# Queries and keys for the block-turned tiles fetched as four consecutive tokens per partition

## The chip, the cores and the metric

The kernel runs on one core of a Trainium2 chip. The metric is device microseconds for one launch. Three runs of the kernel before took 568.88, 570.08 and 571.22 us; the median is 570.08 us. Engines are called by the names of the profile: PE (matrix products; PEld is its weight load), DVE, ACT, POOL, and SP, which here only issues transfers.

## The reference

Eight batches of 576 tokens, eight heads, head width 64. Attention is causal with a window of 128 tokens, a linear distance penalty per head, scale 1/8. Its output, laid out as tokens by 512 features, goes through a gated layer: `h = relu(x @ w_in)` with 1,024 features, a three-tap convolution of `h` along the tokens, `gate = sigmoid(conv)`, and `(h * gate) @ w_out`.

```
scores = scale * q @ k.T ; scores + slope_h * (-|i - j|) where 0 <= i - j < 128, else -1e9
attn   = softmax(scores) ; x = (attn @ v) as [batch, token, head * 64]
h      = max(x @ w_in, 0)
conv   = sum over k of conv_w[k] * h shifted by k - 1 tokens
out    = (h * sigmoid(conv)) @ w_out
```

## The kernel before

All 4,608 tokens are one row of 36 tiles of 128 tokens. A batch has four and a half tiles, so tiles 4, 13, 22 and 31 hold the end of one batch and the start of the next. For tiles 0 to 8 the queries and keys are turned (feature to partition) on PE. For tiles 9 to 35 (`TURN = 9`) they are turned on DVE in blocks of 32 by 32, and the change touches these alone.

For such a tile the steps are, with their names in the written-out order:

- `LD`, `load` and `load_blocks` (lines 281 to 301): SP fetches queries and keys into `raws[t]`. Partition `32 * h + r` of a group of four heads holds, for each of the four blocks `m` of 32 tokens, the 64 features of token `32 * m + r` of head `h`. One transfer per tensor, group and block: 128 pieces of 256 bytes, 16 transfers a tile. Three buffers hold `raws`.
- `TQ`, `turn` (line 348): DVE turns all 32 by 32 blocks, giving `blks[t]`, in which the free index of a row runs over the tile's 128 tokens in order.
- `HQ`, `qk_hi` (line 361): ACT writes the rounded part of all 1,024 values per partition to `qkT`.
- `LQ`, `qk_lo` (line 368): POOL (DVE for tiles 9 and 10) writes what the rounding left to `qkT_low`.
- `S`, `scores_blocks` (line 387): PE forms the scores from `qkT` and `qkT_low`.

Behind them on the engines come: on POOL the normalisation `N` (line 508), `XL` (line 658, which the next up-projection `UH`, line 698, reads), the halves of the gate `GL` (line 767), and the masks `CE` (lines 569, 573) of the probabilities, which go by way of DRAM: `TE` (line 541, DVE), `WE` (line 550, SP writes), `SE` (line 561, SP reads back), `CE`, and then `AV` (line 592) on PE.

The order on every engine, SP among them, is written out by hand: an opening, thirteen periods of two tiles each (tiles 8 and 9, 10 and 11, up to 34; the first at t = 8), a tail. In a period for tiles t and t + 1 SP runs `LD5` (tile t + 5), `WE2`, `SE1`, `SE2`, the values' loads, `LD6`, output stores and `WE3`. `TQ3 HQ3 LQ3` and `TQ4 HQ4 LQ4` prepare tiles t + 3 and t + 4, and `S3.0`, `S4.0` use them in the same period. An engine takes its instructions strictly in this order.

Of the kernel before, what the change touches and what calls it, by code (L numbers as in the profile page):

```python
# [14 lines left out]
ALU = mybir.AluOpType  # L15

P = 128
# [5 lines left out]
def tile_alibi_window_attention_conv_glu(  # L23
# [10 lines left out]
    nc = tc.nc  # L34
# [21 lines left out]
    def as32(ap):  # L56
        return ap.bitcast(F32)
# [21 lines left out]
    def mask_from(name, conds):  # L79
# [19 lines left out]
        out=mh, in_=mh, pattern=[[0, P]], compare_op=ALU.is_ge, fill=0.0, base=-(P // 2), channel_multiplier=1  # L99
# [13 lines left out]
        out=dist, in0=m_prev_f, scalar=float(P), in1=dist, op0=ALU.mult, op1=ALU.add  # L113
# [4 lines left out]
    for h in range(H):  # L118
        slope = 2.0 ** (-8.0 * (h + 1) / H)
        nc.vector.tensor_scalar(  # L120
            out=bias[:, h, :], in0=dist, scalar1=-8.0 * slope, scalar2=None, op0=ALU.mult
# [127 lines left out]
    qkT_low = cpool.tile([P, SLOTS, 2, 2, NG, P], F32R, name="qkT_low")  # L249
    qkTs = {}  # L250

    def qkT_of(t):
        kind = F32 if t < SPLIT else F32R
        if kind not in qkTs:
            qkTs[kind] = apool.tile([P, SLOTS, 2, 2, NG, P], kind, name=f"qkT{t}", tag="qkT", bufs=1)
        return qkTs[kind]
# [11 lines left out]
    def segments(t):  # L268
        g, end = t * P, (t + 1) * P
        while g < end:  # L270
            b, s = divmod(g, S)
            n = min(end - g, S - s)
            yield g - t * P, b, s, n
            g += n

    TURN = 9
    BK = 32
    NB = P // BK
    blks = {}

    def load_blocks(t, dst, src):
        for r, b, s, n in segments(t):
            for g in range(NG):
                for m in range(0, n, BK):
                    nc.sync.dma_start(
                        out=dst[:, g, (r + m) // BK],
                        in_=src[b, g * NB : (g + 1) * NB, s + m : s + m + BK, :],
                    )

    def head_of(t, i):  # L290
        return i if t < TURN else i % 2 + 2 * (i // HU) + NB * (i // 2 % 2)
# [4 lines left out]
    def load(t):  # L296
        if t >= TURN:
            raws[t] = apool.tile([P, 2, NG, NB, D], F32, name=f"rqk{t}", tag="rqk", bufs=3)
            for i, src in enumerate((q, k)):
                load_blocks(t, raws[t][:, i], src)  # L300
            return
        rqk = apool.tile([P, 2, H, D], F32, name=f"rqk{t}", tag="rqk", bufs=3)
        for dst, src in ((rqk[:, 0], q), (rqk[:, 1], k)):
            fetch(t, dst, src)
        raws[t] = [rqk]
# [37 lines left out]
    def turn(t):  # L343
# [6 lines left out]
            in_=raws[t].rearrange("p i g m (b r) -> p (i g) m b r", r=BK),  # L350
        )

    def turned_of(x, t):
        return x[:, t % SLOTS].rearrange("p u i g k -> p (u i g k)").rearrange(
            "p (i g b k) -> p i g b k", i=2, g=NG, k=P
        )

    def qk_hi(t):
        if t < TURN:
            return  # L360
        nc.scalar.copy(out=turned_of(qkT_of(t), t), in_=blks[t])  # L361

    def qk_lo(t):
        if t < TURN:
            return
        hi = as32(turned_of(qkT_of(t), t))
        eng = nc.vector if t in LQ_DVE else nc.gpsimd
        eng.tensor_tensor(out=turned_of(qkT_low, t), in0=blks[t], in1=hi, op=ALU.subtract)  # L368

    def scores_blocks(t):  # L370
        first, slot, win, prev, cur = window(t)
# [456 lines left out]
    def qk_rest(t):  # L828
# [4 lines left out]

    TILE = {
        "LD": load, "LH": load_half, "QU": qkT, "QV": qkT_out, "LV": loadv, "Q": qk, "QO": qk_out, "QL": qk_rest, "QM": qkT_rest, "TE": turn_e, "WE": write_e, "SE": swap_e, "CE": select_e, "TQ": turn, "HQ": qk_hi, "LQ": qk_lo, "MP": place, "MB": add_bias, "KH": keys_hi, "KL": keys_low, "KT": keys_top, "S": scores, "MA": merge,
        "X": lambda t, u, h: exps(t, u, range(h, HU, 2)),
        "NR": recips, "N": normal, "T": attnT, "RL": attn_out, "SEL": select, "AV": av, "XA": x_part, "XS": x_sum, "XH": x_hi, "XL": x_lo, "XF": xfin,
# [107 lines left out]
```

## Time and profile before

| what | value |
|---|---|
| three runs, median | 570.08 us |
| the profiled execution, its own time | 568.98 us |
| its span (first to last instruction) | 567.3 us |
| PE busy | 558.1 us, 98% |
| DVE, ACT, POOL busy | 82%, 76%, 70% |
| hardware transfer queue, share of the 16 engines | 51.6% |

The span is what the trace covers; the profiled execution's own time is 1.7 us longer. A busy share is a mean over the opening, the periods and the tail, and each of them has to be looked at by itself. A group of instructions is told by its line, its engine and the tiles that it writes and reads.

### The profile page before, as it was taken

To read this page: it belongs to the slowest core of one execution; us is meant where nothing else is said; L and a number is where in the kernel's file an instruction comes from. 1 tells how busy PE (TensorE), PEld (TensorE's weight loads), DVE (VectorE), ACT (ScalarE), POOL (GpSimd) and SP (SyncE) were. 2 spreads that over 40 slices of the span, in tenths; PEclk is the share of its full clock that TensorE was granted. 3 is DMA by queue.
4 is the path that set the end of the run, shared out by engine and by line. 5 is a ranking of instruction groups with operands and counts; after the bars stand their busy time and mean duration, and the time that the engine had idled before them with its cause. 6 is when DMAs were issued, how large, how long until landed. Compare 5 with 4: busy or idle time off the path is not lost.

```text
span 567.3 us, 16990 instructions
## 1 busy us (share of the span) xinstructions
PE 558.1 (98%) x6121; PEld 490.0 (86%) x6121; DVE 463.2 (82%) x1474; ACT 430.6 (76%) x1225; POOL 394.8 (70%) x453
## 2 busy tenths in 40 slices
PE   9889999999999999999999999999999999999997
PEld 7667878788989898989898998989898989899996
DVE  7899999999889987888778877788879987765444
ACT  6899988777777878778777877777876888664463
POOL 2667677777878787778677778777677878564141
PEclk9899999999999999999999999999999999999999
DMA  8996813325656474747484647474746462630001
GB/s 196 260 251 138 258 36 76 99 70 160 134 156 139 131 164 125 175 121 173 124 177 124 172 125 174 125 175 125 174 123 171 125 171 79 150 112 25 16 11 66
DMA packets 141225, 76.63 MB, mean 135 GB/s; under 512 B 116412, under 2 KB 131028, under 8 KB 141140
## 3 DMA queue, kind: packets, MB, share of 16 engines
q1 hardware_dynamic: 141140, 75.55, 51.6%
q8 instruction: 48, 0.79, 0.6%
q14 instruction: 37, 0.30, 0.2%
HBM read 51.40 MB, written 24.12 MB: 133 GB/s over the span
## 4 chain that ended last, share of the span: by engine, by line
PE 91%; DVE 4%; DMA 2%; issue 1%; SPq 1%; ACT 0%; DVEq 0%
PE o L801 34%; PE p L698 34%; PE sc L387 8%; PE av L592 7%; PE o L791 2%; DMA rqk<-in_k_dram 2%; PE sc L432 2%; DVE sc L458 1%; PE av L632 1%; PE p L693 1%; SPq L320 1%; DVE wg L216 1%; PE pt L330 1%; DVE e L476 1%; DVE low L209 0%
## 5 line engine op out<-in xcount | busy, mean ns | idle before, releaser
L698 PE MATMUL p<-ring,wi 128*128 128x256 f32 x1088 | 195.4, 281 | 0.0
L731 DVE SCALAR_TENSOR_TENSOR zp<-hh,cw,zp 128x256 f32<-128x256 f32 (+7 forms) x384 | 160.5, 418 | 41.5 <-ACT zp L716 34.0
L698 PEld LDWEIGHTS p<-ring,wi 128*128 128x128 f32 x1088 | 168.7, 188 | 3.3 <-issue 0.2
L698 PE MATMUL p<-ring,wl 128*128 128x256 f32 x544 | 152.3, 280 | 0.0
L767 POOL TENSOR_TENSOR gl<-z,gh 128x512 fp32r<-128x512 f32 x67 | 86.8, 1296 | 79.9 <-ACT gh L758 79.1
L484 ACT ACTIVATE e<-e,st 128x128 f32<-128x128 f32 x288 | 112.7, 394 | 17.7 <-DVE st L476 17.4
L801 PE MATMUL o<-wo,gh 128*128 128x512 f32 x270 | 110.3, 409 | 0.0
L801 PE MATMUL o<-wo,gl 128*128 128x512 f32 x270 | 105.7, 392 | 0.0
L801 PE MATMUL o<-wl,gh 128*128 128x512 f32 x270 | 105.6, 391 | 0.0
L698 PEld LDWEIGHTS p<-ring,wl 128*128 128x128 f32 x544 | 102.7, 189 | 0.0
L716 ACT ACTIVATE zp<-hh,cw 128x256 f32<-128x256 f32 x144 | 68.9, 478 | 30.8 <-DVE z L746 20.2
L508 POOL TENSOR_TENSOR e<-e,st 128x512 f32<-128x512 f32 x60 | 62.4, 1041 | 15.1 <-DVE st L496 14.9
L368 POOL TENSOR_TENSOR qkT_low<-blk,qkT 128x1024 fp32r<-128x1024 f32 x25 | 59.9, 2397 | 16.8 <-ACT qkT L361 10.5
L476 DVE CUSTOM_DVE_ANT_0 e<-sc,bias 128x128 f32<-128x128 f32 x288 | 69.0, 285 | 1.1 <-DVE sc L458 0.2
L738 ACT ACTIVATE zp<-zp 128x512 f32<-128x512 f32 (+1 forms) x73 | 42.1, 577 | 33.3 <-DVE zp L731 33.1
L801 PEld LDWEIGHTS o<-wo,gh 128*128 128x128 f32 x270 | 50.6, 187 | 13.8 <-issue 0.2
L746 DVE SCALAR_TENSOR_TENSOR z<-zp,hh 128x512 f32<-128x512 f32 (+1 forms) x73 | 49.3, 676 | 14.1 <-ACT zp L738 12.3
L801 PEld LDWEIGHTS o<-wo,gl 128*128 128x128 f32 x270 | 50.6, 187 | 11.6
L710 ACT ACTIVATE hh<-p 128x512 f32<-128x512 f32 x67 | 40.0, 597 | 26.2 <-PE p L698 24.1
L801 PEld LDWEIGHTS o<-wl,gh 128*128 128x128 f32 x270 | 50.8, 188 | 9.5
L458 DVE COPY_PREDICATED sc<-m_prev,sc 128x256 f32<-128x256 uint8 x128 | 50.9, 420 | 8.9 <-PE sc L387 6.4
L484 ACT ACTIVATION_READ_ACCUMULATOR e<-e,st 128x1 f32 x288 | 54.3, 188 | 0.0
(124 smaller groups left out, 1071.1 us busy)
## 6 DMA issues: line engine op xcount, KB each, us to landing
scr<-eb SPq DMA_DIRECT2D x28, 512.0 KB
rr<-scr SPq DMA_DIRECT2D x112, 128.0 KB
out_dram<-ob SPq DMA_DIRECT2D x35, 256.0 KB
rv<-in_v_dram SPq DMA_DIRECT2D x32, 256.0 KB
rqk<-in_q_dram SPq DMA_DIRECT2D x216, 32.0 KB
rqk<-in_k_dram SPq DMA_DIRECT2D x216, 32.0 KB
wst<-in_moe_w_in_dram SPq DMA_DIRECT2D x8, 512.0 KB
wst<-in_moe_w_out_dram SPq DMA_DIRECT2D x8, 512.0 KB
```

Of the source, the lines that this page charges most:

```text
L368: eng.tensor_tensor(out=turned_of(qkT_low, t), in0=blks[t], in1=hi, op=ALU.subtract)
L387: nc.tensor.matmul(to, turned_of(tq, t)[rows, 0, g, b], of, start=n == 0, stop=n == len(passes) - 1)
L458: nc.vector.copy_predicated(out=s_cur, mask=mask.unsqueeze(1).to_broadcast(shp), data=data)
L476: nc.vector.tensor_tensor_reduce(out=e[:, j, :], in0=s_cur[:, g, :], in1=bias[:, head_of(t, u * HU + j), :], scale=-0.125, scalar=FAR, op0 ...
L484: nc.scalar.activation(out=e[:, j, :], in_=e[:, j, :], func=AF.Exp, bias=st[:, 0, j : j + 1], scale=-1.0, accum_out=st[:, 1, j : j + 1],)
L508: eng.tensor_tensor(out=e, in0=e, in1=st[:, 2, :].unsqueeze(2).to_broadcast([P, HU, P]), op=ALU.mult)
L698: nc.tensor.matmul(ps, a[:, part], ring[:, i, cc, cols], start=cc == 0 and n == 0, stop=cc == NCC - 1 and n == 2)
L716: nc.scalar.activation(out=zps[s][:, ff, :], in_=hhs[s][:, ff, 1 : 1 + CW], func=AF.Copy, scale=cw[:, 1, f : f + 1])
L731: nc.vector.scalar_tensor_tensor(out=z[:, ff, a:cut], in0=hh[:, ff, a + kk : cut + kk], scalar=cw[:, kk, f : f + 1], in1=z[:, ff, a:cut], ...
L746: nc.vector.scalar_tensor_tensor(out=zgs[s][:, ff], in0=zps[s][:, ff], scalar=1.0, in1=hhs[s][:, ff, 1 : 1 + CW], op0=ALU.add, op1=ALU.mult,)
L767: eng.tensor_tensor(out=gl, in0=zgs.pop(s), in1=as32(gh), op=ALU.subtract)
L801: nc.tensor.matmul(to, a[:, ff, ms], w[:, part], start=first and n == 0, stop=end and n == 2)
```

## The change

The transfers of tiles 9 to 35 take four consecutive tokens to a partition: partition `32 * h + r` now holds tokens `4 * r` to `4 * r + 3` of head `h`, which are 1,024 consecutive bytes in memory. A tile inside one batch takes one transfer per tensor and group of four heads, four in all instead of 16. For the tiles 13, 22 and 31 each batch's half is fetched head by head: 16 partitions to a transfer, 32 transfers a tile. The turn on DVE is unchanged, but its result now holds token `4 * c + m` at place `32 * m + c`. `qk_hi` and `qk_lo` put this right: each is cut in two (queries, then keys), 512 values per partition each, and reads `blks` with a step of 32 values (128 bytes) between neighbours, four of them, then the next column. What they write, and the second operand of `qk_lo`, lie in the order of the tokens as before.

```diff
     def load_blocks(t, dst, src):
         for r, b, s, n in segments(t):
             for g in range(NG):
-                for m in range(0, n, BK):
-                    nc.sync.dma_start(
-                        out=dst[:, g, (r + m) // BK],
-                        in_=src[b, g * NB : (g + 1) * NB, s + m : s + m + BK, :],
-                    )
+                of = src[b, g * NB : (g + 1) * NB, s : s + n, :].rearrange("h (p m) d -> h p (m d)", m=NB)
+                if n == P:
+                    nc.sync.dma_start(out=dst[:, g].rearrange("p m d -> p (m d)"), in_=of)
+                    continue
+                for h in range(NB):
+                    rows = slice(h * BK + r // NB, h * BK + (r + n) // NB)
+                    nc.sync.dma_start(out=dst[rows, g].rearrange("p m d -> p (m d)"), in_=of[h])
...
+    def by_token(blk):
+        return blk.rearrange("p g b (m c) -> p (g b) c m", c=BK)
+
+    def in_order(x):
+        return x.rearrange("p g b (c m) -> p (g b) c m", m=NB)
...
     def qk_hi(t):
         if t < TURN:
             return
-        nc.scalar.copy(out=turned_of(qkT_of(t), t), in_=blks[t])
+        for i in range(2):
+            nc.scalar.copy(out=in_order(turned_of(qkT_of(t), t)[:, i]), in_=by_token(blks[t][:, i]))
 
     def qk_lo(t):
         if t < TURN:
             return
         hi = as32(turned_of(qkT_of(t), t))
         eng = nc.vector if t in LQ_DVE else nc.gpsimd
-        eng.tensor_tensor(out=turned_of(qkT_low, t), in0=blks[t], in1=hi, op=ALU.subtract)
+        for i in range(2):
+            eng.tensor_tensor(
+                out=in_order(turned_of(qkT_low, t)[:, i]), in0=by_token(blks[t][:, i]), in1=in_order(hi[:, i]),
+                op=ALU.subtract,
+            )
```

## Rows read from the trace of the kernel before

**Rows 1.** The page: span, and busy time by engine.
```profile
span 567.3 us, 16990 instructions
...
PE 558.1 (98%) x6121; PEld 490.0 (86%) x6121; DVE 463.2 (82%) x1474; ACT 430.6 (76%) x1225; POOL 394.8 (70%) x453
```

**Rows 2.** Stretches: length, busy time (instructions) per engine, clock, DMA.
```profile
0.00:47.90 47.90, 42.70 (x332) 34.11 (x333) 40.80 (x167) 40.33 (x142) 25.24 (x44) 0.96 0.92 229
47.90:66.70 18.80, 18.38 (x144) 14.76 (x143) 17.81 (x50) 16.76 (x51) 14.81 (x20) 1.00 0.74 196
66.70:492.16 425.46, 425.42 (x5045) 376.93 (x5044) 364.74 (x1173) 334.69 (x955) 324.93 (x352) 1.00 0.54 138
...
302.36:331.42 29.06, 29.06 (x373) 26.12 (x374) 24.36 (x78) 22.46 (x65) 22.91 (x26) 1.00 0.55 146
```

**Rows 3.** The chain that ended last: start, length, what (all on PE).
```profile
134.97 1.62 PE sc L387 x44
...
163.54 1.61 PE sc L387 x39
...
308.17 1.61 PE sc L387 x39
...
452.84 1.61 PE sc L387 x39
...
457.43 5.67 PE p L698 x48
```

**Rows 4.** The timeline of POOL: start, length, instruction, idle time before it.
```profile
131.60 2.40 POOL L368 TENSOR_TENSOR qkT_low<-blk,qkT 128x1024 fp32r<-128x1024 f32 x1 [0.32 <-ACT qkT L361]
...
159.43 2.39 POOL L368 TENSOR_TENSOR qkT_low<-blk,qkT 128x1024 fp32r<-128x1024 f32 x1 [0.30 <-ACT qkT L361]
...
303.59 2.39 POOL L368 TENSOR_TENSOR qkT_low<-blk,qkT 128x1024 fp32r<-128x1024 f32 x1 [0.30 <-ACT qkT L361]
...
437.06 0.72 POOL L569 TENSOR_SCALAR_AFFINE_SELECT ll<-rr 128x512 f32<-128x512 f32 x1
...
449.42 2.40 POOL L368 TENSOR_TENSOR qkT_low<-blk,qkT 128x1024 fp32r<-128x1024 f32 x1 [0.30 <-ACT qkT L361]
...
454.53 1.30 POOL L658 TENSOR_TENSOR ring<-xx,ring 128x512 fp32r<-128x512 f32 x1 [0.45 <-ACT ring L644]
```

**Rows 5.** Groups by line: count, busy us, mean ns of one, idle before.
```profile
L767 POOL TENSOR_TENSOR gl<-z,gh 128x512 fp32r<-128x512 f32 x67 | 86.8, 1296 | 79.9 <-ACT gh L758 79.1 <-POOL hh L768 0.7
...
L508 POOL TENSOR_TENSOR e<-e,st 128x512 f32<-128x512 f32 x60 | 62.4, 1041 | 15.1 <-DVE st L496 14.9
...
L758 ACT CAST gh<-z 128x512 fp32r<-128x512 f32 (+1 forms) x69 | 41.4, 600 | 5.7 <-DVE z L746 5.7
...
L361 ACT CAST qkT<-blk 128x1024 fp32r<-128x1024 f32 x27 | 27.9, 1032 | 0.0
...
L190 ACT ACTIVATE wg<-wst 128x512 f32<-128x512 f32 x9 | 6.1, 673 | 0.0
```

**Rows 6.** The timeline of ACT in a regular period.
```profile
302.48 1.03 ACT L361 CAST qkT<-blk 128x1024 fp32r<-128x1024 f32 x1
...
313.11 0.40 ACT L484 ACTIVATE e<-e,st 128x128 f32<-128x128 f32 x1 [2.12 <-DVE st L476]
```

**Rows 7.** The timeline of SP in the period that fetches tile 31.
```profile
418.53 5.46 SPq L285 DMA_DIRECT2D rqk<-in_q_dram  x8
424.05 4.83 SPq L285 DMA_DIRECT2D rqk<-in_k_dram  x8
428.98 0.48 SPq L550 DMA_DIRECT2D scr<-eb  x1
429.55 5.68 SPq L561 DMA_DIRECT2D rr<-scr  x8
```

**Rows 8.** Issues of stores on SP: count, ns min/median/max, first and last start.
```profile
L818 SPq DMA_DIRECT2D out_dram<-ob x35: 332/376/738, 108.1 to 563.0; - x35
```

**Rows 9.** The timeline of DVE: a turn that waits for its fetch.
```profile
303.74 1.25 DVE L348 STREAM_TRANSPOSE blk<-rqk 128x1024 f32<-128x1024 f32 x1 [0.87 <-DMA out_dram<-ob]
```

## Prediction

> **What bounds the kernel now.** I read the busy times of the page first, then the same times cut into stretches, then the chain of waits, then the timelines of POOL, ACT and SP around the steps that change.
>
> On the page PE is busy for 558.1 of 567.3 us and no other engine over 82% [rows 1]. A mean does not say where the missing 9 us lie, so the reader looks at the stretches [rows 2]: 47.90 - 42.70 = 5.2 us of PE's idle time lie in the first 47.9 us, in which no transfer of the changed kind is issued; 18.80 - 18.38 = 0.42 us between 47.9 and 66.7 us; 425.46 - 425.42 = 0.04 us in all the rest up to 492 us. A regular period lasts 29.06 us and PE fills it. In it DVE has 24.36, ACT 22.46 and POOL 22.91 us of work, so ACT idles 6.6 and POOL 6.15 us a period. The clock stands at 1.00 there.
>
> So whatever the change gives back on SP, DVE or the transfer engines can shorten the kernel by 0.46 us at most, and anything that comes late for PE lengthens it one for one. The question is what comes late. The scores of the period's first tile, S3.0, are the step with the least room: LQ of that tile ends on POOL shortly before PE gets there. The reader subtracts the end of a row of line 368 [rows 4] from the start of the next score row [rows 3]. Regular period: 308.17 - (303.59 + 2.39) = 2.19 us. Of it about 0.1 us is the handing on of the result (line 361 ends at 302.48 + 1.03 = 303.51, line 368 starts at 303.59 [rows 4, 6]), so the room is 2.1 us. The same sum gives 0.88 us for tile 11 (131.60 and 134.97), 1.63 us for tile 13 (159.43 and 163.54), and 0.93 us for tile 33 (449.42 and 452.84). Tile 13 stands for three (13, 21, 31), tile 33 for two (15, 33), the regular one for seven; with tile 11 these are the thirteen odd tiles. The even tiles have more room: two down-projections and an up-projection of PE stand between their LQ and their scores.
>
> **The change part by part.**
>
> *Transfers.* SP issues 16 transfers a tile in 5.46 + 4.83 = 10.3 us [rows 7]; four take about a quarter, so SP gains some 7.5 us a tile. DVE's turn of the second tile, which waits up to 0.87 us for its fetch [rows 9], no longer waits. Both lie beside a full PE: worth 0 to 0.46 us; I take 0. The bytes are the same, and a load is issued a whole period before its turn, so how fast it runs does not matter.
>
> *The three divided tiles.* They take 32 issues where 16 stood. An issue costs 0.38 us by the stores' median [rows 8] and 0.60 us by the present loads (4.83 / 8 [rows 7]): 12.2 to 19.2 us, 1.9 to 8.9 us more than now. Tiles 13 and 31 are fetched by LD5, ahead of WE2 and SE1 in SP's order, so the probabilities come back later by that. SE1's first four reads now end near 429.55 + 5.68 / 2 = 432.4 us, and the mask that needs them starts at 437.06 [rows 4, 7]: 4.7 us, part of which is the landing. POOL has 12.4 us from there to LQ of tile 33 at 449.42, of which by its share in a period (6.15 of 29.06) some 2.6 us are idle, an estimate. A delay up to some 5 us is therefore swallowed, the upper end would leave 2 us. I take 0, near the stores' row, because the pieces are fewer than in any transfer shown.
>
> *The cut of HQ.* One instruction of 1,032 ns becomes two of 600 ns, the price of the same cast at half the length [rows 5]; they overlap by some 0.1 us in the queue, so +0.07 us if the step of 128 bytes costs nothing. Streaming 512 values takes 1,032 - 600 = 432 ns; if ACT read at half rate, 0.86 us would be added, +0.93 us in all. Below nothing it can't go: no work is taken off ACT. The only row with a step is line 190, which reads every second word (8 bytes) at 673 ns against 600 [rows 5], +0.07 us per 512. It stands near the lower end, but nothing stands near the upper one, so I take the middle, +0.5 us.
>
> *The cut of LQ.* One instruction of 2.39 us becomes two of 1.30 us [rows 4, 5]; with some 0.1 us of overlap, +0.12 us. The step comes on top, on one operand of two. Line 508, whose second operand is one value repeated, takes 1,041 ns against 1,296 ns for line 767 with two full ones [rows 5]: the way in which one operand is read is worth 0.255 us per 512, 0.51 us per tile. I take that again, +0.63 us. Ends: +0.12 us (the step is free) and +2.3 us (the streaming, 2 x (2.39 - 1.30) = 2.2 us a tile, doubles).
>
> *Sum.* LQ ends 0.5 + 0.63 = 1.13 us later after HQ. That exceeds the room of tile 11 by 0.25 us and of tiles 15 and 33 by 0.2 us each; everywhere else it fits. PE loses 0.65 us. Queued behind LQ on POOL are N and two XL, which UH needs: in the period of tile 33 the second XL ends at 454.53 + 1.30 = 455.8 us and UH starts at 457.43 [rows 3, 4], 1.6 us of room against 1.13 and later still by PE's own 0.2. Behind HQ on ACT the delay ends where ACT waits for DVE, 2.12 us in the regular period [rows 6]. Tiles 9 and 10 pay their LQ on DVE, once, without a row for it; I take nothing. The profiled execution took 568.98 us, so 569.6; the median of the three runs is 1.10 us above it, so **570.7 us**.
>
> [...] No row shows what a step of 128 bytes costs on ACT or POOL; the row with 8 bytes shows +0.07 us [rows 5]. [...]
>
> **The rivals.**
>
> *Half rate on both engines: slower.* ACT streams its reads at half rate (+0.93 us) and POOL pays as much for the stepped operand as half its streaming (+1.1 + 0.12 us): 2.15 us. It decides from 0.88 us on, and from 2.1 us every odd tile stalls PE. Losses: 1.27 (tile 11), 2 x 1.22 (15, 33), 3 x 0.52 (13, 21, 31), 7 x 0.05: 5.6 us, so 574.6 and as a median 575.7 us. For it: every value that the two engines read lies 128 bytes from the last. [...]
>
> *POOL's streaming doubles: much slower.* +0.93 and +2.3 us give 3.25 us: 2.4 + 2 x 2.3 + 3 x 1.6 + 7 x 1.15 = 19.9 us, 590 us as a median. POOL would still fit its period (22.91 + 4.6 = 27.5 of 29.06). Against: one operand alone is stepped.
>
> *The divided tiles hold up the masks: slightly slower.* At 0.60 us an issue, two periods lose up to 2 us each; with the 1.13 us, 573 to 575 us.
>
> *The freed SP and DVE make it faster.* It would need PE to wait for a transfer after 47.9 us; the stretches leave 0.46 us for that [rows 2], 569.6 us as a median. That the loads are not faster at all would give the forecast's time too.
>
> **How the numbers follow.** Forecast 0.50 (up to some 2.5 us of loss; its own range 569.0 to 572.9). Half rate 0.33. POOL doubled 0.06. Divided tiles 0.06. A gain 0.05. No change and a change under 0.5% (2.85 us) can't be told apart here. Faster 0.04, from the gain and the scatter of the runs; slower: half rate, POOL doubled and part of the divided tiles, 0.42; within 0.5%: 0.54. The range takes in the half-rate case with its spread and leaves out the doubled POOL: 568.9 to 578.0 us.
>
> **What the profile will show.** The group of line 361's successor: two casts of 128x512 per tile, near 0.6 us if the step is free, 0.85 as I take it, over 1.0 at half rate. On POOL two of 128x512, 1.3 us if free, 1.6 as forecast, 1.85 at half the streaming more. The scores of tiles 11, 15 and 33 should show PE idle by a few tenths, waiting for the new LQ; seven more such waits mean the first rival. SP should idle for over 10 us a period, and the turn should no longer wait for a fetch. In the periods of tiles 13 and 31 the masks of the first tile start late if the 32 issues cost 0.6 us. The forecast is wrong if PE's idle time after 47.9 us grows by over 3 us, or if 48 up-projections take less than their 5.67 us [rows 3] with fewer packets about.

## The result and the profile after

The change costs 0.7%: ratio 1.0068, 95% interval 1.0043 to 1.0094 (median 573.7 us over eight runs, 569.66 us for the kernel before, timed beside it). The profiled execution took 573.24 us, 4.26 us more than the one of before. The forecast was 570.7 us with 568.9 to 578.0 us as its range.

The page, span and busy time by engine, after (before: [rows 1]):

```profile
span 571.5 us, 16761 instructions
...
PE 561.1 (98%) x6121; PEld 492.0 (86%) x6121; DVE 463.9 (81%) x1476; ACT 458.3 (80%) x1252; POOL 412.8 (72%) x478
```

ACT has 27.7 us more work, POOL 18.0, DVE 0.7. The stretches after, with the columns of [rows 2]; the last is that of 66.70 to 492.16 us before, its ends moved with PE's work:

```profile
0.00:47.90 47.90, 43.15 (x328) 34.38 (x328) 40.30 (x166) 39.89 (x141) 25.07 (x43) 0.96 0.90 226
47.90:66.70 18.80, 18.40 (x145) 14.84 (x144) 17.87 (x49) 16.82 (x51) 15.10 (x20) 1.00 0.88 228
67.18:496.86 429.68, 427.45 (x5045) 378.10 (x5044) 365.35 (x1176) 362.26 (x982) 342.36 (x377) 1.00 0.49 135
```

The same 5,045 matrix products that took 425.46 us [rows 2] take 429.68 us: the 4.2 us by which the span grew lie there, with the clock at 1.00. The row shows 2.23 us of PE idle in place of 0.04; the other 2 us are in PE's busy time, because the records of the products overlap and the last one before a wait runs on into it (at tile 11 PE's products stop for 1.02 us, of which 0.64 us is recorded as idle). I therefore compare the start of each stretch of PE's work with the same stretch of before, and call a *step* a place where the difference jumps. The steps after: +1.02 us at the scores of tile 11, +0.46 (12), +0.23 (15), +0.34 (16), +1.88 (21), +0.23 (33), +0.28 (34), 4.4 us in all; between them PE keeps pace to 0.1 us.

The groups of the changed instructions after (count, busy us, mean ns of one, idle before; before: [rows 5]):

```profile
L780 POOL TENSOR_TENSOR gl<-z,gh 128x512 fp32r<-128x512 f32 x67 | 87.6, 1307 | 58.0 <-ACT gh L771 57.2 <-POOL hh L781 0.7
L378 POOL TENSOR_TENSOR qkT_low<-blk,qkT 128x512 fp32r<-128x512 f32 x50 | 78.4, 1594 | 18.6 <-ACT qkT L370 18.5
...
L370 ACT CAST qkT<-blk 128x512 fp32r<-128x512 f32 x54 | 58.9, 1140 | 0.0
L771 ACT CAST gh<-z 128x512 fp32r<-128x512 f32 (+1 forms) x69 | 41.5, 601 | 4.8 <-DVE z L759 4.8
...
L350 DVE STREAM_TRANSPOSE blk<-rqk 128x1024 f32<-128x1024 f32 x27 | 33.5, 1240 | 7.6 <-DMA rqk<-in_k_dram 7.5
```

The same cast of 128x512 takes 1,140 ns stepped and 601 ns contiguous, so a tile's pair holds ACT for 2.19 us in place of 1.03. POOL's step costs 1,594 - 1,307 = 287 ns per 512. And the turn on DVE now waits 7.5 us for transfers, nearly all of it at tiles 14 (1.67 us), 22 (4.81) and 32 (1.07): the divided tile 22, and the two whose fetch comes next behind a divided one.

**The small steps.** The chain of waits after, at the scores of tile 11 (start, length, what):

```profile
133.93 0.48 ACT xx L626
134.41 0.50 ACT hh L723
134.91 0.48 ACT ring L664
135.39 0.02 issue
135.42 0.70 DVE ring L673
136.12 0.04 issue
136.16 1.68 PE sc L400 x40
```

ACT, late behind its casts, hands its part of the up-projection's input to DVE late; DVE's `ring` is the last reader of a PSUM buffer (a buffer that PE writes its products to) that the scores take next. PE has issued three products of the scores at 135.14 and then stands until 136.16. POOL had finished the low parts of that tile at 131.94 + 3.15 = 135.09, before PE came to them.

The other small steps have the same origin, by other buffers; PE always stops before a product of the rounded parts, not of the low ones. At tile 12 DVE waits for ACT (`zp`), and behind that gives back the scores of tile 11 late:

```profile
145.32 0.69 DVE L759 SCALAR_TENSOR_TENSOR z<-zp,hh 128x512 f32<-128x512 f32 x1 [0.31 <-ACT zp L751]
...
146.77 0.08 DVE L489 DVE_READ_ACCUMULATOR2_ANT st<- 128x1 f32 x1
```

PE's third product of tile 12 starts at 146.91 us; tiles 16 and 34 show the same, 0.06 us behind DVE's line 489. At tiles 15 and 33 ACT itself gives the buffer back. Tile 15, where PE goes on at 194.53 us:

```profile
193.87 0.60 ACT L723 ACTIVATE hh<-p 128x512 f32<-128x512 f32 x1
```

POOL's low parts of tile 15 end at 194.2 us, 0.3 us before PE goes on.

**The large step.** SP, DVE and PE after, around the turn of tile 22:

```profile
260.52 10.16 SPq L290 DMA_DIRECT2D rqk<-in_q_dram  x16
270.73 8.27 SPq L290 DMA_DIRECT2D rqk<-in_k_dram  x16
```

```profile
281.33 1.25 DVE L350 STREAM_TRANSPOSE blk<-rqk 128x1024 f32<-128x1024 f32 x1 [4.81 <-DMA rqk<-in_k_dram]
282.50 0.13 DVE L509 RECIPROCAL st<-st 128x4 f32<-128x4 f32 x1
282.55 0.65 DVE L619 TENSOR_TENSOR xx<-xx,av 128x512 f32<-128x512 f32 x1
```

```profile
283.26 0.38 PE L400 MATMUL sc<-qkT 32*128 32x256 f32 x2 [1.51 <-DVE xx L619]
```

The 32 transfers of the divided tile hold SP from 260.52 to 279.00 us. The turn starts 2.3 us behind the last issue, DVE has stood for 4.81 us, and what is queued behind the turn on DVE frees a PSUM buffer that PE's scores of tile 21 wait for. Before, SP had issued this tile's 16 transfers in 9.5 us:

```profile
263.63 4.92 SPq L285 DMA_DIRECT2D rqk<-in_q_dram  x8
268.60 4.49 SPq L285 DMA_DIRECT2D rqk<-in_k_dram  x8
```

Even so the turn waited a little for them:

```profile
275.04 1.25 DVE L348 STREAM_TRANSPOSE blk<-rqk 128x1024 f32<-128x1024 f32 x1 [0.83 <-DMA rqk<-in_k_dram]
```

**The masks.** In the periods that fetch tiles 13 and 31 the 32 issues stand ahead of the read-back of the probabilities, and the masks are late. The mask of the first of these periods, before and after:

```profile
148.71 0.72 POOL L573 TENSOR_SCALAR_AFFINE_SELECT rr<-rr 128x512 f32<-128x512 f32 x1
```

```profile
153.02 0.72 POOL L586 TENSOR_SCALAR_AFFINE_SELECT rr<-rr 128x512 f32<-128x512 f32 x1 [2.26 <-DMA rr<-scr]
```

PE is 1.77 us later itself there, so the mask is late by 2.5 us. In the period of tile 31 it starts at 415.93 in place of 407.95 us, 3.8 us more than PE's own 4.19. In experiment 1, without the 32 issues, the same two masks keep within 0.65 us of PE's own shift. PE shows no step in either period.

### The profile page after: what moved, and what is told of

It reads as the page before. It is cut to its first block, busy times and chain, and to the rows that moved or that the text cites. A ratio compares the mean times of both kernels' runs of the same rounds, so it can differ in the third digit from the quotient of the medians.

```text
span 571.5 us, 16761 instructions
## 1 busy us (share of the span) xinstructions
PE 561.1 (98%) x6121; PEld 492.0 (86%) x6121; DVE 463.9 (81%) x1476; ACT 458.3 (80%) x1252; POOL 412.8 (72%) x478
## 2 busy tenths in 40 slices
DMA packets 99942, 76.61 MB, mean 134 GB/s; under 512 B 61308, under 2 KB 89748, under 8 KB 99860
## 3 DMA queue, kind: packets, MB, share of 16 engines
q1 hardware_dynamic: 99860, 75.55, 48.1%
## 4 chain that ended last, share of the span: by engine, by line
PE 83%; DVE 8%; SPq 3%; DMA 2%; ACT 2%; issue 1%; DVEq 0%; ACTq 0%
PE p L711 31%; PE o L814 30%; PE sc L400 7%; PE av L605 6%; SPq L290 3%; PE o L804 2%; PE sc L445 2%; DVE sc L471 1%; DMA rqk<-in_k_dram 1%; DVE e L489 1%; DVE zp L744 1%; DMA rqk<-in_q_dram 1%; PE p L706 1%; PE pt L332 1%; DVE wg L216 1%
## 5 line engine op out<-in xcount | busy, mean ns | idle before, releaser
L780 POOL TENSOR_TENSOR gl<-z,gh 128x512 fp32r<-128x512 f32 x67 | 87.6, 1307 | 58.0 <-ACT gh L771 57.2
L378 POOL TENSOR_TENSOR qkT_low<-blk,qkT 128x512 fp32r<-128x512 f32 x50 | 78.4, 1594 | 18.6 <-ACT qkT L370 18.5
L370 ACT CAST qkT<-blk 128x512 fp32r<-128x512 f32 x54 | 58.9, 1140 | 0.0
```

What stands on the lines that cost most here:

```text
L370: nc.scalar.copy(out=in_order(turned_of(qkT_of(t), t)[:, i]), in_=by_token(blks[t][:, i]))
L378: eng.tensor_tensor(out=in_order(turned_of(qkT_low, t)[:, i]), in0=by_token(blks[t][:, i]), in1=in_order(hi[:, i]), op=ALU.subtract,)
L780: eng.tensor_tensor(out=gl, in0=zgs.pop(s), in1=as32(gh), op=ALU.subtract)
```

## The experiments

Ratios are to the kernel before, with the 95% interval. Theory at the start: the divided tile makes some 2 us of the loss, ACT's stepped casts the rest. "Before, plus" kernels hold one part of the change alone.

### 1. The divided tiles as before

The halves of tiles 13, 22 and 31 are fetched as before, and their turned values read contiguously.

```diff
+                if n < P:
+                    for m in range(0, n, BK):
+                        nc.sync.dma_start(
+                            out=dst[:, g, (r + m) // BK],
+                            in_=src[b, g * NB : (g + 1) * NB, s + m : s + m + BK, :],
+                        )
+                    continue
...
+        if len(list(segments(t))) > 1:
+            nc.scalar.copy(out=turned_of(qkT_of(t), t), in_=blks[t])
+            return
...
```

> The changed kernel, but tiles 13, 22 and 31 are fetched, turned and read as before (16 transfers, one cast, one subtraction). Theory C (the 32 transfers of tile 22 hold up its turn on DVE by 4.8 us, and DVE then frees a score buffer late): the wait of the turn goes, PE's offset no longer steps by 1.9 us at tile 21, and the time falls by 1.9 us to about 571.8 us. Rival (that step comes from the stepped reads like the others): the step stays and the time stays near 573.7 us.

Measured: 571.46 us, ratio 1.0021 [1.0005, 1.0037]. The step of 1.88 us at tile 21 is gone, the six small ones stand to within 0.05 us of their size. The turn of tile 22 in this run, without a wait:

```profile
276.56 1.23 DVE L357 STREAM_TRANSPOSE blk<-rqk 128x1024 f32<-128x1024 f32 x1
```

The divided tiles' part is shown.

### 2. ACT's cast contiguous

```diff
-        for i in range(2):
-            nc.scalar.copy(out=in_order(turned_of(qkT_of(t), t)[:, i]), in_=by_token(blks[t][:, i]))
+        nc.scalar.copy(out=turned_of(qkT_of(t), t), in_=blks[t])
```

> The changed kernel, but HQ is one cast of 1,024 values read in a row, as before; the tokens of qkT are then out of order, so the scores are of permuted tokens and only the time counts. Theory A (ACT, late by two casts of 1.14 us, lets DVE free score buffers late): the steps at tiles 11, 12, 15, 16, 33 and 34, 2.6 us in all, go; with the divided tile left, about 571.2 us. Theory B (POOL's subtraction comes late): LQ still takes 3.1 us, so about 1 us or less goes, 573 us.

Measured: 572.7 us, 1.0045 [1.0023, 1.0067]; the theory said 571.2. Its profiled execution (576.35 us) shows no step at tiles 11, 12, 16, 33 and 34, as the theory has it. At tile 15 0.27 us stays, and that one is POOL's: the low parts end at 196.29 us, and PE's first product of them starts at 196.35. The execution also shows a new step of 1.2 us at tile 10, one of 0.8 us at tile 13 (the turn of tile 14, fetched behind the divided tile 13, waits 2.87 us) with 0.3 us more up to tile 15, and at tile 21 steps of 3.0 and 1.1 us in place of 1.88. The stretches of that run around tile 21 (columns of [rows 2]):

```profile
283.00:285.00 2.00, 0.16 (x2) 0.00 (x0) 1.62 (x3) 0.00 (x0) 0.23 (x1) 1.00 0.40 126
285.00:287.00 2.00, 1.68 (x44) 1.68 (x46) 1.96 (x5) 1.40 (x3) 1.81 (x2) 0.84 0.27 97
287.00:289.00 2.00, 2.00 (x11) 1.49 (x7) 1.95 (x6) 1.55 (x4) 1.57 (x2) 0.50 0.68 252
289.00:291.00 2.00, 2.00 (x8) 1.59 (x8) 1.96 (x12) 2.00 (x7) 1.22 (x1) 0.80 0.90 269
```

PE stood for nearly all of 283 to 285 us, and behind that the granted clock fell to 0.50 (287 to 289 us) and came back within some 4 us. This wait was paid twice. In time, the run alone did not decide for ACT; 9 to 12 take the parts one by one.

### 3. POOL's low parts contiguous

```diff
-        for i in range(2):
-            eng.tensor_tensor(
-                out=in_order(turned_of(qkT_low, t)[:, i]), in0=by_token(blks[t][:, i]), in1=in_order(hi[:, i]),
-                op=ALU.subtract,
-            )
+        eng.tensor_tensor(out=turned_of(qkT_low, t), in0=blks[t], in1=hi, op=ALU.subtract)
```

> The changed kernel, but LQ is one subtraction of 1,024 values read in a row, as before, against a qkT in token order, so the low parts are of other tokens and only the time counts. Theory A: nothing changes but tiles 15 and 33 at most, 573.3 us. Theory B: the steps at 11, 15 and 33 go, 1.5 us, 572.2 us.

Measured: 574.57 us, 1.0072 [1.0046, 1.0099], no faster than the whole change. All steps stay, that of tile 11 at 1.00 us, with POOL back at its old time and ACT's casts stepped:

```profile
L377 POOL TENSOR_TENSOR qkT_low<-blk,qkT 128x1024 fp32r<-128x1024 f32 x25 | 60.1, 2403 | 43.4 <-ACT qkT L370 35.1 <-DVE st L485 6.1 <-DVE zp L740 2.2
L370 ACT CAST qkT<-blk 128x512 fp32r<-128x512 f32 x54 | 58.4, 1130 | 0.0
```

POOL's longer instructions are not the cause. The run does not make the low parts earlier, though: in one instruction they have to wait for both casts.

```profile
134.03 2.40 POOL L377 TENSOR_TENSOR qkT_low<-blk,qkT 128x1024 fp32r<-128x1024 f32 x1 [1.43 <-ACT qkT L370]
```

They end at 136.43 us in place of 135.09, with PE 1.04 us later itself. That PE did not wait for them is read from the trace: it goes on at 137.20 us, behind DVE's `ring`. At tiles 15 and 33 they end within 0.01 us of ACT's `hh`, so there this run does not tell the two apart; the whole change, where they end 0.25 to 0.3 us before it, does. The step of tile 33 is larger here, 0.7 us, behind DVE's line 615 (`xx`), late in this execution. That this run is somewhat over its expected time lies inside its interval.

### 4. The transfers alone

The edits of 2 and 3 together: the new transfers, the old casts and low parts.

```diff
+        nc.scalar.copy(out=turned_of(qkT_of(t), t), in_=blks[t])
...
+        eng.tensor_tensor(out=turned_of(qkT_low, t), in0=blks[t], in1=hi, op=ALU.subtract)
```

> The changed kernel with HQ and LQ both as before: only the transfers are changed (tokens out of order, only the time counts). Theories A and B together with C: only the step of the divided tile 22 is left, 1.9 us, 571.6 us; every other step is gone. If freeing SP and DVE is worth something it shows here as less than 1.9 us over the kernel before.

Measured: 571.6 us, 1.0024 [1.0006, 1.0042]. No step at tiles 11, 12, 15, 16, 33, 34. The loss of the divided tiles is there without any stepped access. In the profiled execution (570.41 us) it fell on the turn of tile 14, whose fetch follows the divided tile 13 on SP: a wait of 2.74 us and a step of 0.86 us, while the turn of tile 22 waited 2.40 us without a step. So the place of this loss differs between executions.

### 5. The stepped accesses alone

Before, with the new `qk_hi` and `qk_lo`.

```diff
-        nc.scalar.copy(out=turned_of(qkT_of(t), t), in_=blks[t])
+        for i in range(2):
+            nc.scalar.copy(out=in_order(turned_of(qkT_of(t), t)[:, i]), in_=by_token(blks[t][:, i]))
...
-        eng.tensor_tensor(out=turned_of(qkT_low, t), in0=blks[t], in1=hi, op=ALU.subtract)
+        for i in range(2):
+            eng.tensor_tensor(
+                out=in_order(turned_of(qkT_low, t)[:, i]), in0=by_token(blks[t][:, i]), in1=in_order(hi[:, i]),
+                op=ALU.subtract,
+            )
```

> The kernel before with the change's two casts and two subtractions with a step of 128 bytes; the transfers are those of before, so tokens end out of order and only the time counts. Theory (ACT's late casts let DVE free score buffers late, apart from the transfers): PE's offset steps at tiles 11, 12, 15, 16, 33 and 34, some 2.5 us in all, none at 21: 572.3 us. Rival (the freed SP and DVE of the change had been paying part of it back): steps larger than in the run with the divided tiles as before, 573 us or more.

Measured: 571.69 us, 1.0024 [1.0007, 1.0041]. The six small steps (1.02, 0.46, 0.23, 0.34, 0.20, 0.35) without the large one. The two halves of the change lose 0.24% each, together 0.48%, within the interval of the whole. Against experiment 1, which differs by the new transfers of the 24 whole tiles (and reads the three divided ones contiguously), there is no difference that can be measured: a quarter of the transfers gives SP some 7 us a tile (9.4 to 10.4 us of issues become 2.3 to 3.2), and that gains nothing here.

### 6. The step on the writing side

Experiment 1, with contiguous reads and writes that step by 16 bytes.

```diff
+    def in_blocks(blk):
+        return blk.rearrange("p g b (m c) -> p (g b) m c", c=BK)
+    def spread(x):
+        return x.rearrange("p g b (c m) -> p (g b) m c", m=NB)
...
-            nc.scalar.copy(out=in_order(turned_of(qkT_of(t), t)[:, i]), in_=by_token(blks[t][:, i]))
+            nc.scalar.copy(out=spread(turned_of(qkT_of(t), t)[:, i]), in_=in_blocks(blks[t][:, i]))
...
```

> Divided tiles as before; in the others HQ and LQ read blks in a row and write (LQ also reads qkT) with a step of 16 bytes instead. If only stepped reads are dear: casts of 0.6 us, time as before the change, 569.9 us. [...]

Measured: 570.64 us, 1.0006 [0.9986, 1.0027], no measurable loss. But the cast is not cheaper by its mean:

```profile
L386 ACT CAST qkT<-blk 128x512 fp32r<-128x512 f32 x48 | 49.9, 1143 | 0.0
```

A pair takes 2.10 us in place of 2.19. The steps at tiles 15, 16, 33 and 34 are under 0.1 us, those of 11 and 12 are 0.79 and 0.20 us; all six are 0.1 to 0.3 us smaller than in experiment 1. Why 0.1 us less on ACT should take off up to 0.3 us I could not settle; the interval overlaps that of experiment 1, so in time the two are not told apart.

### 7. The order put right by the turn

DVE writes with a step of 16 bytes, casts and low parts are contiguous, and the divided tiles are treated as before.

```diff
-            out=blks[t].rearrange("p i g b (m c) -> p (i g) m b c", c=BK),
+            out=(
+                blks[t].rearrange("p i g b (m c) -> p (i g) m b c", c=BK)
+                if len(list(segments(t))) > 1
+                else blks[t].rearrange("p i g b (c m) -> p (i g) m b c", m=NB)
+            ),
...
```

> Divided tiles as before; DVE's turn writes the tokens in order (a step of 16 bytes on its output), HQ and LQ are the single instructions of before. If DVE's turn is not slowed by the step, nothing comes late: 569.9 us, and at best 0.4 us less, since PE has no more idle time to give. If the turn takes twice as long (2.4 us), DVE is late by 2.4 us a period and PE waits for score buffers in the periods in which DVE is fullest: 571 to 573 us.

Measured: 570.89 us, 1.0007 [0.9988, 1.0026]. DVE pays instead of ACT and POOL:

```profile
L357 DVE STREAM_TRANSPOSE blk<-rqk 128x1024 f32<-128x1024 f32 x27 | 53.5, 1981 | 0.0
L380 ACT CAST qkT<-blk 128x1024 fp32r<-128x1024 f32 x27 | 27.9, 1034 | 1.6 <-DVE blk L357 1.6
```

The mean of 1,981 ns mixes two forms: the turns of the three divided tiles, left as they were, take 1.24 us, the other 24 2.03 to 2.17 us, so (53.5 - 3 x 1.24) / 24 = 2.07 us. A stepped turn takes 0.83 us more. ACT waits for it three times, 1.6 us in all; steps of 0.68 (tile 11), 0.43 (15) and 0.45 us (33) remain, and the time cannot be told from that of before, short of the 571 to 573 us that I expected of a turn twice as long. So the new transfers of the whole tiles gain nothing that can be measured in this form either.

### 8. ACT's time without a step

Before, with each cast done twice, contiguously.

```diff
-        nc.scalar.copy(out=turned_of(qkT_of(t), t), in_=blks[t])
+        for i in range(2):
+            for _ in range(2):
+                nc.scalar.copy(out=turned_of(qkT_of(t), t)[:, i], in_=blks[t][:, i])
```

> The kernel before, with HQ as four casts of 512 values read in a row (each half written twice): about 2.0 us of ACT a tile, as the stepped pair takes 2.2, and nothing else changed. Theory (it is the time on ACT, not the step nor POOL): the same steps at tiles 11, 12, 15, 16, 33, 34, some 2 us in all, 571.9 us. Rival (the step disturbs DVE or PE in another way): no steps, 569.9 us.

Measured: 574.03 us, 1.0063 [1.0039, 1.0087]. Four casts of 615 ns, 2.43 us a tile:

```profile
L363 ACT CAST qkT<-blk 128x512 fp32r<-128x512 f32 x108 | 63.9, 615 | 1.7
```

The same six steps, larger: 1.28, 0.69, 0.82, 0.57, 0.82, 0.56. Time on ACT alone makes the pattern, whatever the access. It costs more than the 571.9 us expected since it is longer (2.43 against 2.19 us): four steps are 0.2 to 0.3 us larger than after the change, and those of 15 and 33 0.6 us, because there PE waits for DVE's line 608 (`xx`) first. The low parts have to wait for all four casts, but PE did not wait for them at tile 11, where they end at 135.25 us and PE goes on at 136.04.

### 9. ACT's step alone

Before, with the new `qk_hi` alone.

```diff
-        nc.scalar.copy(out=turned_of(qkT_of(t), t), in_=blks[t])
+        for i in range(2):
+            nc.scalar.copy(out=in_order(turned_of(qkT_of(t), t)[:, i]), in_=by_token(blks[t][:, i]))
```

> The kernel before, with its transfers, and only the casts of the queries and keys cut in two and stepped (their values come out of order; the low parts are taken in one contiguous instruction). Theory, ACT alone makes the stepped accesses' share of the loss: ACT pays 2.19 us a tile, POOL 2.39 us as before, PE has new waits for score buffers at tiles 11, 12, 15, 16, 33 and 34, and the time is 1.5 to 2.5 us over the kernel before (571.2 to 572.2 us). Rival, ACT and POOL together make it: with POOL at its old length the low parts end 0.75 us earlier than with both, the waits at 15, 33 and the even tiles are gone, and at most 1 us is lost (to 570.7 us).

Measured: 571.66 us, 1.0030 [1.0011, 1.0048]. Six steps, 1.01, 0.43, 0.23, 0.29, 0.21 and 0.31 us, 2.5 in all. The theory's number and its tiles: ACT's stepped casts are enough for them. My rival was badly set, for the low parts do not end earlier here but later, as in experiment 3: at tile 11 at 135.54 us, 0.23 us after PE's first score product, where in the whole change they end 0.05 us before it. PE goes on at 136.33 us, behind DVE's `ring`.

### 10. The stepped low parts alone

Before, with the new `qk_lo` alone.

```diff
-        eng.tensor_tensor(out=turned_of(qkT_low, t), in0=blks[t], in1=hi, op=ALU.subtract)
+        for i in range(2):
+            eng.tensor_tensor(
+                out=in_order(turned_of(qkT_low, t)[:, i]), in0=by_token(blks[t][:, i]), in1=in_order(hi[:, i]),
+                op=ALU.subtract,
+            )
```

> The kernel before, with its transfers, and only the low parts of the queries and keys cut in two and stepped (their values come out of order; the casts are one contiguous instruction). Theory, ACT alone: POOL pays 3.14 us a tile in place of 2.39, 0.75 us more, which fits into the room that every odd tile has (0.88 us at the least), and the time is that of the kernel before within 0.3 us (569.7 us). Rival, both: tiles 11, 15 and 33 lose some tenths each, 0.5 to 1 us in all.

Measured: 572.51 us, 1.0052 [1.0031, 1.0072]. Neither theory: no step at tiles 11, 15 or 33, but one of 3 us at tile 10. DVE, POOL and PE of that run (with the idle time before and what ended it):

```profile
111.18 3.09 DVE L375 TENSOR_TENSOR qkT_low<-blk,qkT 128x512 fp32r<-128x512 f32 x2
```

```profile
111.47 1.90 POOL L777 TENSOR_TENSOR gl<-z,gh 128x512 fp32r<-128x512 f32 x1
```

```profile
118.91 1.22 PE L397 MATMUL sc<-qkT 32*128 32x256 f32 x4 [1.16 <-DVE st L486]
```

Tiles 9 and 10 have their low parts taken by DVE. Beside an instruction of POOL the pair takes 3.09 us; in experiment 5, where ACT's later casts make POOL start at 112.24 us, the same pair takes 2.13 us. Behind the wait of 1.16 us the clock falls to 0.50:

```profile
119.00:121.00 2.00, 1.96 (x43) 1.67 (x47) 1.93 (x15) 1.85 (x10) 1.85 (x3) 0.99 0.00 0
121.00:123.00 2.00, 2.00 (x16) 1.58 (x11) 1.94 (x6) 1.29 (x6) 0.68 (x1) 0.50 0.00 0
123.00:125.00 2.00, 2.00 (x7) 1.52 (x6) 1.91 (x11) 1.89 (x9) 1.16 (x2) 0.65 0.00 0
```

The same pair of 3.09 us and a wait of 1.17 us make the new step of experiment 2 at tile 10, the other run with contiguous casts and stepped low parts; there the clock stayed at 1.00 behind that wait.

### 11 and 12. POOL's 25 tiles, and DVE's two, by themselves

The kernel of 10, with this ahead of the loop; in 12 the condition reads `t not in LQ_DVE`.

```diff
+        if t in LQ_DVE:
+            eng.tensor_tensor(out=turned_of(qkT_low, t), in0=blks[t], in1=hi, op=ALU.subtract)
+            return
```

> The kernel before, with only the low parts of the 25 tiles that POOL takes cut in two and stepped (their values come out of order); those of tiles 9 and 10 are taken by DVE in one contiguous instruction as before. Theory, the low parts cost time only where DVE takes them: POOL's 0.75 us more a tile meet no waiting PE, no step appears in PE's progress, 569.7 us as the kernel before, ratio within 0.2%. Rival, POOL's share costs something after all: steps at tiles 11, 15 and 33, 570.3 to 571 us.

> The kernel before, with only the low parts of tiles 9 and 10, the two that DVE takes, cut in two and stepped (their values come out of order). Theory, these two make the whole loss of the run with all low parts stepped: DVE takes 3.1 us for each beside an instruction of POOL, the scores of tile 10 start 1.2 us late, PE's granted clock falls to 0.50 for some 3 us behind that, and 2.5 to 3 us are lost (572.2 to 572.7 us). Rival, POOL's 25 tiles make it: 569.7 us.

Measured: 570.37 us, 1.0001 [0.9982, 1.0020], for POOL's tiles; 570.68 us, 1.0009 [0.9994, 1.0024], for DVE's. POOL's share costs nothing that can be measured, and the interval of DVE's takes in no loss too. In the profiled execution of 11 there are steps of 0.7 us (tile 31) and 0.8 us (tile 33), but they stand behind late fetches of the old kind, as two turns on DVE show; so the old transfers can be late too:

```profile
422.98 1.25 DVE L348 STREAM_TRANSPOSE blk<-rqk 128x1024 f32<-128x1024 f32 x1 [3.64 <-DMA rqk<-in_k_dram]
...
452.91 1.25 DVE L348 STREAM_TRANSPOSE blk<-rqk 128x1024 f32<-128x1024 f32 x1 [1.28 <-DMA out_dram<-ob]
```

DVE's two tiles make the wait at tile 10 again, 1.4 us of steps in the profiled execution, and lose less than I expected. PE and the stretches of run 12:

```profile
118.55 1.23 PE L400 MATMUL sc<-qkT 32*128 32x256 f32 x4 [1.15 <-DVE st L489]
```

```profile
119.00:121.00 2.00, 1.95 (x48) 1.62 (x47) 1.89 (x12) 2.00 (x11) 1.93 (x3) 1.00 0.00 0
121.00:123.00 2.00, 2.00 (x10) 1.67 (x10) 1.88 (x6) 1.22 (x5) 0.48 (x2) 1.00 0.00 0
```

The same wait as in 10, but the clock stays at 1.00. What made it fall in 10 at tile 10 and in 2 at tile 21 is open; no run tells it. So in the profiled execution the loss of 10 is the wait at tile 10 and the clock behind it, and not POOL. The medians are not explained by this: 11 and 12 together lose 0.1% and 10 loses 0.5%, and whether the clock fell in the other executions of 10 is not shown. In the whole change this wait does not arise.

## Why the prediction was right, and where it was not

The time was inside the range, 3.0 us over the forecast (570.7 us) and 2.0 us under the half-rate rival (575.7 us). It lies above the forecast's own range (to 572.9 us), and the range held because it was drawn out for half rate; neither of the two mechanisms that made the loss, ACT's queue and the turn of tile 22, was in the sum. That the number was met is in this part luck. By its steps:

- **PE bounds, freed resources give nothing.** Right. The new transfers of the whole tiles, with some 7 us less of SP's time a tile, left 1.0021 [1.0005, 1.0037] in experiment 1 against 1.0024 [1.0007, 1.0041] in experiment 5, and after the change, with 99,860 packets in place of 141,140, 48 up-projections take 5.67 us as before.
- **"A load is issued a whole period before its turn, so how fast it runs does not matter."** This step failed. It never held for the even tiles, which `LD6` fetches: before, SP's last issue for tile 22 ended at 268.60 + 4.49 = 273.09 us and DVE's turn, which waited 0.83 us for it, started at 275.04. With 32 pieces SP finished tile 22's at 279.00 us, and DVE wanted them at 276.5. The row that I had cited myself, a turn waiting 0.87 us [rows 9], was the warning.
- **"The divided tiles: I take 0"**, with the masks of tiles 13 and 31 as the risk. The issues of tile 22 cost 18.43 / 32 = 0.58 us, near the upper price, those of 13 and 31 0.51 and 0.54 us. The masks came 2.5 and 3.8 us late, as feared, and PE lost nothing by it, as I had said of delays up to some 5 us. But the rows that I worked this out from are of the wrong period: those of [rows 7] and the mask at 437.06 us belong to the fetch of tile 33, while before the change tile 31 was issued from 389.46 to 399.42 us. The bill, 1.9 us, came by the turn of tile 22 on DVE, which I did not price.
- **HQ, "I take the middle, +0.5 us".** Mis-sized: +1.16 us a tile, beyond the upper end of +0.93. Streaming 512 values takes 1,140 - 168 = 972 ns where 601 - 168 = 433 ns stood, if the fixed part is 168 ns in both (600 - 432, by [rows 5]): the step then more than doubles it, an estimate. The row with a step of 8 bytes (+73 ns) did not show what a step of 128 bytes costs.
- **LQ, +0.63 us.** Nearly right: 3.15 - 2.39 = +0.76 us, 1,594 ns an instruction where 1.6 us was forecast.
- **Sum and place.** I added the two, 1.13 us, and set the sum against LQ's room. Wrong in mechanism. POOL starts after the first half of ACT's pair, so LQ of tile 11 ended only 135.09 - 134.00 = 1.09 us later [rows 4], of which 0.25 us is the opening's shift of PE: 0.84 us against a room of 0.88 us. The low parts stayed just in time, and the seven regular periods did not stall. What was late was ACT itself: "behind HQ on ACT the delay ends where ACT waits for DVE" holds in the regular period, not in the first one (tiles 11 and 12) and those of tiles 15, 16 and of 33, 34, where ACT's next work frees PSUM buffers, itself or by way of DVE. Experiments 8 and 9 show that ACT's time is enough for it, 11 that POOL's longer instructions alone do not make it; that PE waits for ACT's work and not for the low parts is read from the traces. Tiles 11, 15 and 33 were named; 12, 16 and 34, which I had given more room, stalled too.
- **Half rate on both engines** came nearest, for another reason than its own: ACT paid more than it said and POOL less, and of its 13 stalls three came, none of them by the low parts. Half rate was my assumption, and no run shows its terms, +0.93 us on ACT and +1.1 us for POOL's step: after the change ACT pays +1.16 us a tile, and POOL's step costs 2 x 0.287 = 0.57 us.
- **"PE's idle time after 47.9 us grows by over 3 us"**, the sign that the forecast is wrong: PE's recorded idle time from 66.7 us on grew by 2.2 us, its progress lost 4.4 us. Read from the steps, the sign was there.

By PE's steps, the stepped casts lose 2.5 us (experiment 9; 2.6 in 5) and the divided tile 1.9 us (after, and gone in 1), 4.4 us together, which is the sum of the steps after. What stays open: why the steps of experiment 6 are so small, why 11 and 12 do not add up to 10, when the clock falls behind a wait, and what makes a fetch late in one execution and not in the next.

## What to carry to other kernels

Price a change of layout on the engine that reads the result, not only on the transfers: here a step of 128 bytes nearly doubled a cast (601 to 1,140 ns), and nothing was to be had for the saved transfers because PE hardly waited for anything (0.04 us idle from 66.7 to 492 us [rows 2]). When a step gets longer, follow what is queued behind it on its own engine to the next buffer that the full engine needs; the step's own reader may still be served in time. And count the issues of the odd tiles: four transfers where sixteen stood does not help if one tile in nine needs thirty-two, just ahead of its use (a step of 1.88 us at tile 21 here).

## What the runs showed of the hardware

- A cast of 128x512 on ACT takes 601 ns contiguous, 1,140 ns with reads 128 bytes apart, 1,143 ns with writes 16 bytes apart (experiment 6). The step on the write was as dear as that on the read.
- The 32x32 turn of 1,024 values on DVE takes 1,240 ns, and 2.07 us when its writes lie 16 bytes apart (experiment 7).
- DVE's stepped subtraction of two operands took 2.13 us a pair with POOL idle for most of it and 3.09 us beside a subtraction of POOL (experiments 5, 10, 12; experiment 2 has the 3.09 us too).
- An issue of a load on SP cost about the same in two shapes: 18.43 / 32 = 0.58 us for 16 partitions of 1 KB, 0.59 us (9.41 / 16) for 128 pieces of 256 bytes. The stores' took 0.38 us [rows 8].
- A wait of PE of 1.16 us was followed by 2 us at a granted clock of 0.50 and 2 us at 0.65 in one run (experiment 10), and a wait of 1.15 us at the same place was not in another (12, clock 1.00), nor was one of 1.51 us at tile 21 after the change. The length of the wait alone does not tell.
